# A new order for every engine's work in a fused attention and gated-FFN kernel, with each engine's line of tasks taken strictly in turn

## The chip, the cores and the metric

The kernel runs on one core of a Trainium2 chip. The core has a matrix engine (TensorE, PE; its weight loads are shown apart as PEld), a vector engine (VectorE, DVE), a scalar engine (ScalarE, ACT), a general engine (GpSimd, POOL) and an engine that here only issues DMAs (SyncE, SP). The metric is the device time of one execution in microseconds; a lower time is better.

## The reference

```python
def _attn_ref(q, k, v, centroids):          # q, k, v: 4 x 8 x 768 x 64; centroids: 8 x 16 x 64
    q_n, k_n, c_n = (each row divided by its norm + 1e-06)
    q_assign = np.argmax(np.einsum('bhsd,hcd->bhsc', q_n, c_n), axis=-1)
    k_assign = np.argmax(np.einsum('bhsd,hcd->bhsc', k_n, c_n), axis=-1)
    mask = q_assign[:, :, :, None] == k_assign[:, :, None, :]
    scores = 1 / np.sqrt(D) * np.matmul(q, k.transpose(0, 1, 3, 2))
    scores = np.where(mask, scores, -1000000000.0)
    attn = softmax(scores)                  # with the maximum taken off, sum + 1e-09
    return np.matmul(attn, v)

def reference(...):
    x = attn_out.transpose(0, 2, 1, 3).reshape(3072, 512)
    gate = 1.0 / (1.0 + np.exp(-(x @ w_gate)))     # w_gate, w_val: 512 x 1536
    return gate * (x @ w_val) @ w_out              # w_out: 1536 x 512
```

(Each line that stands for several is shortened.) Every query and key belongs to the nearest of 16 centroids of its head; a query attends to the keys of its own centroid. The result, 3072 tokens of 512 values, goes through a gated feed-forward layer.

## The kernel before

**Attention.** The eight heads are taken as four pairs `p` for each of the four batches `b`. Queries and keys of a pair are loaded in their natural layout (`nat`), turned on PE or DVE into `t` (`t32`), and scored against the centroids (`scored`, L794 on PE); DVE finds the best centroid of each token, and a one-hot mask (`oh`, `oht`) is copied by SP's DMAs into rows beside the turned values in `even` and `odd` (one tile for the even, one for the odd half of the blocks; POOL casts the values into them in L757, and SP copies a part of one to the other in L761). So one matmul of 80 rows (L1114, `score`) gives a score that already carries the mask. For each group of score blocks PE writes scores into two PSUM banks, ACT takes the exponential of both (L1138, `exponentials`, into `es`), and PE multiplies them with the values and a column of ones (L1165, `value`). DVE divides by the sums (L1190 `rec`, L1195 `norm`, into `xn`), and the block is turned into `x` either on PE or by a DMA transposition that SP issues (L1223, `turn_by_dma`).

**Feed-forward.** As soon as a group of 384 tokens has all its pairs, the feed-forward products on it are interleaved with the attention of the next groups. Part of the products with `w_gate` and `w_val` is plain (L1506), part goes through a scheme of seven products for a 2 x 2 block multiplication (`seven_products`, L1584), with sums on DVE (L1615, L1631) and copies and gate functions on ACT (L1603, L1622). The gated values are in `hT`. The product with `w_out` (`project`) also uses seven products (L1375): DVE forms sums of `hT` (L1345), ACT halves some results (L1393, `half` and `diff`), DVE combines a product with one of these into the output tile (L1400, `summed`), and SP or ACT stores the tile (a DMA of L441). In the last group of the program the last product is split in two halves of columns, copied out by ACT (L1393) and DVE (L684) and stored apart.

**Buffers.** The eight PSUM banks are one pool, `ring`: any task that needs a bank or a pair gets one that is free by the plan. `nat` has nine buffers, `es` and `xn` four each, `x`, `hT`, `gt` and `out2` two each. Which buffer a task gets is settled in the plan too; a task that takes a buffer waits for the last users of it.

**What sets the order.** The program is built once as a list of 2390 tasks (`Order.add`): each is a small piece of work on one engine, with the tasks it depends on and the buffers it takes. `Order.run` gives each task its place from a table of numbers (`PLACES`) and each of the 198 DMAs a time from issue to landing that the plan is to count with (`LANDINGS`). `Order.schedule` then plans all engines on one clock: again and again it takes, of all engines, the task that can start first; among the tasks of an engine that could start within 0.02 us of each other it takes the one with the lowest place. The tasks are emitted in that order, and each engine works through its own instructions in the order in which they were emitted, waiting where an input or a buffer isn't ready. No time of the plan is used on the chip; only the orders and the choice of buffers are.

```python
first = min(c[0] for c in cand)
start, t = min(
    (c for c in cand if c[0] <= first + 0.02), key=lambda c: (c[1].due, c[0])
)
if best is None or start < best[0]:
    best = (start, t)
```

For the kernel before, this choice gives on every engine the order of the numbers in `PLACES`.

Of the kernel before, what the change touches and what calls it, by code (L numbers as in the profile page):

```python
# [18 lines left out]
107 121 225 233 263 268 495 255 502 7 22 24 26 30 25 29 35 41 28 33 38 46 34 39 44 50 42 48 53 57 61 64 65 70 76 78  # L19
81 86 45 51 49 55 54 59 56 62 63 68 77 85 75 89 94 100 134 140 142 145 148 166 156 84 110 88 114 95 122 119 129 127  # L20
138 144 153 141 155 162 176 186 189 192 202 207 213 226 124 131 161 174 164 180 183 191 188 197 205 215 201 217 224
234 240 246 251 254 258 264 266 103 109 116 198 187 267 190 270 222 278 248 282 250 291 271 295 279 304 285 312 275
286 297 305 319 325 321 384 389 403 407 357 368 381 411 415 423 445 451 458 468 476 484 328 367 380 418 336 426 434
441 344 450 457 470 525 543 532 538 514 521 530 536 551 561 629 631 556 563 571 576 636 656 652 661 669 675 680 681
660 666 671 677 683 687 695 704 707 688 691 718 700 66 67 69 73 102 71 72 74 79 104 80 82 83 87 106 90 91 93 96 112
120 125 130 98 99 105 132 108 111 113 137 117 118 123 139 126 128 136 149 133 135 143 160 146 147 152 175 200 203
209 150 151 154 157 158 159 163 212 167 168 170 171 172 173 185 214 223 230 235 177 179 181 182 194 236 193 195 196
199 204 237 206 208 210 211 216 239 245 249 252 218 219 220 221 227 253 228 229 231 232 238 256 241 242 243 244 247
262 269 273 283 287 257 259 260 261 265 281 272 274 276 277 280 293 288 289 290 292 294 314 320 322 335 340 353 360
480 488 352 358 366 378 382 386 385 400 399 410 404 416 412 422 421 432 433 442 443 453 454 466 467 477 481 490 489  # L30
496 500 507 506 511 522 528 529 535 534 539 537 542 541 548 546 555 553 560 559 566 296 298 299 300 301 302 306 331
307 308 309 310 311 313 315 332 339 342 347 317 318 323 348 327 329 333 349 337 338 341 359 343 345 351 365 355 356
362 377 361 363 369 383 387 396 401 370 372 373 374 375 376 379 402 388 390 391 392 393 394 398 409 414 420 430 395
397 405 429 406 408 413 431 417 419 425 440 424 427 435 452 437 438 446 465 447 449 455 479 483 486 491 459 460 461
462 463 464 469 497 471 472 473 474 475 478 482 498 501 504 516 519 485 487 492 512 493 494 499 513 503 505 508 520
509 510 515 527 517 518 523 533 524 526 531 540 544 547 552 558 549 569 612 620 568 575 574 580 595 602 630 637 640
647 648 653 625 644 645 650 579 585 587 606 605 611 621 627 658 670 686 690 668 678 673 685 682 694 703 716 693 720
698 725 679 696 689 705 711 724 722 730 573 582 588 591 594 596 598 600 603 570 608 614 618 717 727 729 731 736 734
742 744 751 758 756 762 769 774 784 795 738 753 743 766 772 773 782 778 796 783 797 805 806 814 813 820 827 833 818
931 793 807 810 816 856 865 881 872 890 878 891 899 901 909 915 920 945 957 925 963 632 659 676 646 639 684 649 654  # L40
662 672 713 697 721 726 749 732 699 701 708 712 746 747 785 789 706 715 942 759 798 935 841 857 866 874 885 889 861
# [82 lines left out]
2.47 2.47 2.57 2.47 2.47 2.47 2.47 2.484 2.95 2.95 2.95 2.95 2.95 2.95 2.95 3 2.95 2.95 2.95 2.95 2.95 2.95 2.95  # L124
2.95 2.919 2.9 2.47 2.52 2.484 2.47 2.484 2.47 2.47 2.47 2.8 3.064 2.8 2.8 4.1 4.264 4.1 4.1 3.07 3.204 2.8 2.85 2.8
2.8 4.17 4.17 4.63 4.77 3.07 3.07 3.07 3.07 2.8 2.8 2.8 2.8 3.598 3.07 2.8 2.8 2.8 4.694 4.3 3.07 3.237 3.07 2.735
2.735 2.895
"""


# [1692 lines left out]
```

## Time and profile before

| what | before |
|---|---|
| median of 3 runs | 311.02 us (309.73 to 311.69) |
| profiled execution | 309.38 us, span 307.6 us |
| PE busy | 299.2 us, 97% of the span |
| ACT busy | 259.0 us, 84% |
| DVE busy | 249.3 us, 81% |
| POOL busy | 79.2 us, 26% |
| granted TensorE clock | 1.000 over the span |
| HBM traffic | 28.87 MB read, 6.29 MB written |

The profile is that of one execution; its span runs from the first to the last event that the profiler saw, and the execution's own time is 1.78 us longer. A busy time counts an engine's instructions, so an engine that waits is idle; matmuls overlap in a pipeline and their ends are modelled, so a busy PE can still hide short stalls. Lines are those of the kernel before. In rows of instructions, `out<-in` names the tiles written and read, with the numbers of their buffers left out.

### The profile page before, as it was taken

To read this page: it belongs to the slowest core of one execution; us is meant where nothing else is said; L and a number is where in the kernel's file an instruction comes from. 1 tells how busy PE (TensorE), PEld (TensorE's weight loads), DVE (VectorE), ACT (ScalarE), POOL (GpSimd) and SP (SyncE) were. 2 spreads that over 40 slices of the span, in tenths; PEclk is the share of its full clock that TensorE was granted. 3 is DMA by queue.
4 is the path that set the end of the run, shared out by engine and by line. 5 is a ranking of instruction groups with operands and counts; after the bars stand their busy time and mean duration, and the time that the engine had idled before them with its cause. 6 is when DMAs were issued, how large, how long until landed. Compare 5 with 4: busy or idle time off the path is not lost.

```text
span 307.6 us, 8905 instructions
## 1 busy us (share of the span) xinstructions
PE 299.2 (97%) x3491; PEld 237.5 (77%) x3491; DVE 249.3 (81%) x604; ACT 259.0 (84%) x449; POOL 79.2 (26%) x112
## 2 busy tenths in 40 slices
PE   7998899999999999999999999999999999999994
PEld 3676588754468688977998779987998889988974
DVE  4999996897886687889789989979778738964993
ACT  4898799884448899999999989999999998995841
POOL 5898849741022033600001301470000000000000
PEclk9999999999999999999999999999999999999999
DMA  6999999994557595931384674893210120131003
GB/s 222 368 287 181 218 202 145 181 137 85 97 90 160 111 128 166 118 47 22 84 134 90 104 119 118 178 124 29 71 37 26 40 61 34 25 74 70 0 3 136
DMA packets 97833, 34.79 MB, mean 113 GB/s; under 512 B 83152, under 2 KB 93568, under 8 KB 97792
## 3 DMA queue, kind: packets, MB, share of 16 engines
q1 hardware_dynamic: 72192, 24.57, 34.6%
q0 software_dynamic: 24880, 8.92, 29.2%
q10 hardware_dynamic: 720, 0.75, 0.7%
q8 instruction: 27, 0.44, 0.6%
q14 instruction: 14, 0.11, 0.1%
HBM read 28.87 MB, written 6.29 MB: 114 GB/s over the span
## 4 chain that ended last, share of the span: by engine, by line
PE 89%; ACT 4%; DVE 3%; DMA 2%; issue 1%; ACTq 0%; SPq 0%
PE ring L1584 25%; PE ring L1114 19%; PE ring L1375 18%; PE ring L1506 11%; PE ring L1165 10%; ACT es L1138 3%; PE ring L794 3%; DMA nat<-in_q_dram 1%; PE ring L902 1%; DVE hT L1631 1%; DMA out<-in_centroids_dram 1%; DVE t L684 1%; PE ring L942 1%; DVE even L681 0%; ACT t L909 0%
## 5 line engine op out<-in xcount | busy, mean ns | idle before, releaser
L1138 ACT ACTIVATE es<-ring,nbias 128x768 f16<-128x768 f32 (+1 forms) x189 | 169.8, 941 | 15.1 <-PE ring L1114 10.5
L1165 PEld LDWEIGHTS <-es 128*128 128x128 f16 x1152 | 51.3, 97 | 11.7 <-ACT es L1138 0.8
L1165 PE MATMUL ring<-vp,es 128*128 128x65 f16 x1152 | 56.6, 193 | 0.0
L757 POOL CAST even<-t 128x768 f16<-128x768 f32 x24 | 21.1, 892 | 116.3 <-issue 37.3
L1615 DVE TENSOR_TENSOR nat<-ring,nat 128x384 f32<-128x384 f32 x68 | 36.7, 552 | 14.9 <-ACT nat L1603 8.6
L1622 ACT ACTIVATE nat<-nat 128x384 f32<-128x384 f32 x68 | 37.3, 575 | 1.9 <-DVE nat L1615 1.9
L1584 PEld LDWEIGHTS <-wss 128*128 128x128 f16 x408 | 34.8, 98 | 2.2 <-issue 0.2
L1603 ACT COPY nat<-ring 128x384 f32<-128x384 f32 x68 | 33.9, 519 | 2.7 <-PE ring L1584 1.7
L1584 PE MATMUL ring<-nat,wv 128*128 128x192 f16 x272 | 32.6, 246 | 0.0
L1584 PE MATMUL ring<-nat,wss 128*128 128x192 f16 x272 | 32.4, 246 | 0.0
L1584 PE MATMUL ring<-x,wg 128*128 128x192 f16 x272 | 32.3, 246 | 0.2 <-DVE hT L1631 0.2
L1375 PEld LDWEIGHTS <-hT 128*128 128x128 f16 x294 | 27.2, 97 | 4.9 <-DVE hT L1631 0.4
L1375 PE MATMUL ring<-wo,hT 128*128 128x256 f16 x216 | 29.0, 272 | 0.1
L1114 PE MATMUL ring<-even 80*128 80x384 f16 (+2 forms) x120 | 26.4, 294 | 0.9 <-ACT es L1138 0.6
L1114 PE MATMUL ring<-even,odd 80*128 80x384 f16 (+2 forms) x120 | 26.8, 293 | 0.0
L1114 PE MATMUL ring<-odd 80*128 80x384 f16 x96 | 26.5, 325 | 0.1
L1114 PE MATMUL ring<-odd,even 80*128 80x384 f16 x96 | 26.4, 326 | 0.2 <-ACT es L1138 0.2
L1584 PEld LDWEIGHTS <-wv 128*128 128x128 f16 x272 | 23.3, 97 | 3.0 <-issue 0.2
L1114 PEld LDWEIGHTS <-even 80*128 80x128 f16 x216 | 19.5, 98 | 7.1 <-issue 3.5
L1114 PEld LDWEIGHTS <-odd 80*128 80x128 f16 x216 | 19.3, 98 | 6.6 <-issue 4.5
L1584 PEld LDWEIGHTS <-wg 128*128 128x128 f16 x272 | 23.1, 98 | 1.5 <-issue 0.4
L1506 PE MATMUL ring<-x,wg 128*128 128x256 f16 (+2 forms) x112 | 22.5, 326 | 0.1
(120 smaller groups left out, 519.0 us busy)
## 6 DMA issues: line engine op xcount, KB each, us to landing
out_dram<-out SPq DMA_DIRECT2D x22, 256.0 KB, 2.4
nat<-in_k_dram SPq DMA_DIRECT2D x32, 96.0 KB, 3.1
nat<-in_q_dram SPq DMA_DIRECT2D x32, 96.0 KB, 3.0
odd<-even SPq DMA_DIRECT2D x12, 192.0 KB, 3.5
vp<-in_v_dram POOLq DMA_DIRECT2D x24, 96.0 KB, 5.2
nat<-in_k_dram SPq DMA_DIRECT2D x5, 384.0 KB, 6.2
nat<-in_q_dram SPq DMA_DIRECT2D x5, 384.0 KB, 5.7
nat<-in_v_dram SPq DMA_DIRECT2D x4, 384.0 KB, 7.2
```

The lines of the kernel that those rows point to most:

```text
L684: nc.vector.tensor_scalar(to, of, by, None, ALU.mult)
L757: nc.gpsimd.tensor_copy(t[:, NM[nm], cols], t32[p, nm].tile[:, cols])
L794: nc.tensor.matmul(out=ps[32 * g : 32 * g + 32, half, :QB], lhsT=cblk[:, 2 * p + half, :], rhs=t32[p, nm].tile[:, half * QB : (half + 1) * ...
L1114: nc.tensor.matmul(out=to, lhsT=kb.tile[0:80, 0, e * QB + j // 2 * 128 : e * QB + (j // 2 + 1) * 128], rhs=qb_.tile[0:80, 1, e * QB + c0 * ...
L1138: i = nc.scalar.activation(to, of, AF.Exp, bias=nbias, scale=D ** -0.5 if quarters(b, p) else scale,).ins
L1165: nc.tensor.matmul(out=av.tile[:, g : g + D + 1], lhsT=es.tile[:, i * N + c * 128 : i * N + (c + 1) * 128], rhs=vp[:, e, j, :], start=firs ...
L1375: nc.tensor.matmul(out=ps[:, lo:hi], lhsT=left_()[:, i], rhs=right(i)[:, lo:hi], start=new and i == 0, stop=i == NFC // 2 - 1, skip_group_ ...
L1506: nc.tensor.matmul(out=ps[:, :N], lhsT=ws[fc // FPG][:, dcc, fc % FPG, :], rhs=xb.tile[:, dcc, :N], start=(dcc == 0), stop=(dcc == NDC - 1),)
L1584: nc.tensor.matmul(out=ps[:, f], lhsT=w_[:, d, f], rhs=x_()[:, d], start=new and not (f or d), stop=d == 1, skip_group_check=True,)
L1603: nc.scalar.copy(held(i), bank(r_))
L1615: lambda: nc.vector.tensor_tensor(held(i), bank(r_), held(i), ALU.add), deps,
L1622: lambda: nc.scalar.activation(held(i), held(i), AF.Tanh, scale=0.5), [m], due_ffn(work), lat=0.16,
```

## The change

The two tables are replaced, and three additions in `Order.schedule` let an engine take only the task that is next in its own line, sorted by `PLACES`; the choice by planned start is left only between engines. The numbers of `PLACES` come from a search over such orders in the plan, in which half of the weight was on plans with randomly lengthened transfers; `LANDINGS` holds new times for the plan. No task, instruction or buffer is added or taken away.

```diff
 PLACES = """
 0 1 9 2 16 3 5 10 11 13 14 15 17 19 20 32 36 4 8 6 12 18 21 23 27 92 97 31 37 40 101 115 43 47 52 165 169 58 178 184
-107 121 225 233 263 268 495 255 502 7 22 24 26 30 25 29 35 41 28 33 38 46 34 39 44 50 42 48 53 57 61 64 65 70 76 78
+107 121 214 233 257 282 493 289 455 7 22 24 26 30 25 29 35 41 28 33 38 46 34 39 44 50 42 48 53 57 61 64 65 70 76 78
...
         free = {e: 0.7 for e in {t.eng for t in self.tasks}}
+        line = {e: deque() for e in free}
+        for t in sorted(self.tasks, key=lambda t: t.due):
+            line[t.eng].append(t)
         order, under_way, pool, twin = [], {"SP": [], "POOL": []}, (0.0, 0.0), (0.0, 0.0)
         while any(wait.values()):
             best = None
             for e, ts in wait.items():
                 cand = []
                 for t in ts:
+                    if t is not line[e][0]:
+                        continue
                     r = t.ready
...
             wait[t.eng].remove(t)
+            line[t.eng].popleft()
             now = max(t.ready, free[t.eng])
```

The code of the tasks stays as it was; its lines have moved by four (L1400 before is L1404 in the changed kernel, L1114 is L1118, L441 is L445). On every engine the order is the same in the two kernels up to about 24 us of the profile of before; behind that 413 of PE's 1048 tasks, 354 of DVE's 584, 105 of ACT's 453, 51 of POOL's 107 and 150 of SP's 198 have another place, most on PE and ACT by one or two.

Three places show how. The first is PE's line at about 28 us: transpositions by `ident` (L724, changed L728), scores (L1114, changed L1118) and values (L1165, changed L1169). Before:

```order
L1114 LDWEIGHTS odd2_82
L1114 MATMUL ring_121<-even2_76,odd2_82 128x256
L724 MATMUL ring_121<-ident_124,nat4_65 128x128 x3
L724 MATMUL ring_121<-ident_124,nat5_66 128x128 x3
L1165 LDWEIGHTS es3_98
L1165 MATMUL ring_121<-vp2_142,es3_98 128x65
```

Changed:

```order
L728 MATMUL ring_121<-ident_124,nat4_65 128x128 x3
L1118 LDWEIGHTS even3_77
L1118 MATMUL ring_121<-even3_77 128x256
L1118 LDWEIGHTS even3_77
L1118 MATMUL ring_121<-even3_77 128x256
L1118 LDWEIGHTS even3_77
L1118 MATMUL ring_121<-even3_77 128x256
L1118 LDWEIGHTS odd3_83
L1118 MATMUL ring_121<-even3_77,odd3_83 128x256
L728 MATMUL ring_121<-ident_124,nat5_66 128x128 x3
L1169 LDWEIGHTS es3_98
L1169 MATMUL ring_121<-vp2_142,es3_98 128x65
```

The four scores of the next block (`even3`, `odd3`) now stand between the two transpositions and ahead of the values of `es3`; before they followed those values.

The second is SP's line at about 125 us: masks copied from `oht` into `even` and `odd`, DMA transpositions of the normalized blocks `xn` (L1223, changed L1227), and copies of `even` into `odd` (L761, changed L765). Before:

```order
L441 DMA even2_76<-oht0_86 16x768
L441 DMA odd3_83<-oht0_86 16x768
L441 DMA even2_76<-oht0_86 16x768
L1223 DMA_TRANSPOSE x1_107<-xn2_104 128x3x128
L761 DMA odd4_84<-even5_79 64x1536
L761 DMA odd5_85<-even4_78 64x1536
```

Changed:

```order
L1227 DMA_TRANSPOSE x1_107<-xn0_102 128x3x128
L1227 DMA_TRANSPOSE x1_107<-xn2_104 128x3x128
L445 DMA odd3_83<-oht0_86 16x768
L445 DMA even3_77<-oht0_86 16x768
L445 DMA even2_76<-oht0_86 16x768
L1227 DMA_TRANSPOSE x1_107<-xn1_103 128x3x128
L445 DMA even3_77<-oht0_86 16x768
L765 DMA odd4_84<-even4_78 64x1536
```

All eight masks stood ahead of the transposition of `xn2` before; now four of them stand behind it.

The third is the end of DVE's line: the last sums of `hT` (L1345, changed L1349), the sums into the output tile (L1400, changed L1404) and the last copy. Before:

```order
L1345 TENSOR_TENSOR hT1_109<-hT1_109 128x3x128
L1400 SCALAR_TENSOR_TENSOR out20_112<-ring_121,half0_117 128x256
L1345 TENSOR_TENSOR hT1_109<-hT1_109 128x3x128
L1400 SCALAR_TENSOR_TENSOR out21_113<-ring_121,nat4_65 128x256
L1400 SCALAR_TENSOR_TENSOR out20_112<-ring_121,diff0_118 128x256
L1400 SCALAR_TENSOR_TENSOR out21_113<-ring_121,nat4_65 128x256
L684 TENSOR_SCALAR out21_113<-ring_121 128x128
```

Changed:

```order
L1349 TENSOR_TENSOR hT1_109<-hT1_109 128x3x128
L1349 TENSOR_TENSOR hT1_109<-hT0_108,hT1_109 128x3x128
L1349 TENSOR_TENSOR hT1_109<-hT1_109 128x3x128
L1404 SCALAR_TENSOR_TENSOR out20_112<-ring_121,diff0_118 128x256
L1404 SCALAR_TENSOR_TENSOR out21_113<-ring_121,nat4_65 128x256
L1404 SCALAR_TENSOR_TENSOR out20_112<-ring_121,half0_117 128x256
L1404 SCALAR_TENSOR_TENSOR out21_113<-ring_121,nat4_65 128x256
L688 TENSOR_SCALAR out21_113<-ring_121 128x128
```

The sum with `half0`, and the one of `out21` that stood behind it, complete two output tiles of 256 KB; they have moved behind the sums with `diff0` and with the other `nat4`. The stores on SP keep their order.

204 rows, old and new, of tables (LANDINGS, PLACES) are left out of this document.

## The prediction

> **What bounds the kernel now.** I read the page first: the busy shares, the clock, and the chain of work that ended last.
>
> ```profile
> span 307.6 us, 8905 instructions
> PE 299.2 (97%) x3491; PEld 237.5 (77%) x3491; DVE 249.3 (81%) x604; ACT 259.0 (84%) x449; POOL 79.2 (26%) x112
> PEclk9999999999999999999999999999999999999999
> PE 89%; ACT 4%; DVE 3%; DMA 2%; issue 1%; ACTq 0%; SPq 0%
> ```
>
> TensorE is busy for 299.2 of 307.6 us at a clock that never falls, and 89% of the chain is its own work. No matmul is added or removed, so a new order can only change the 8.4 us in which PE is idle, and whatever stalls hide inside "busy". Where the idle time lies comes from the busy time of each stretch (columns: time, PE, PEld, DVE, ACT, POOL with the count of instructions, then the clock, the DMA share, GB/s).
>
> ```profile
> 24.00:42.00 18.00, 16.02 (x230) 12.00 (x229) 16.86 (x48) 14.98 (x18) 13.60 (x18) 1.00 1.12 204
> 42.00:120.00 78.00, 78.00 (x833) 54.61 (x832) 61.34 (x147) 60.37 (x96) 24.69 (x31) 1.00 0.97 134
> 120.00:240.00 120.00, 119.77 (x1507) 101.81 (x1504) 104.28 (x235) 115.60 (x213) 20.46 (x25) 1.00 0.58 86
> 240.00:296.00 56.00, 55.90 (x655) 48.56 (x654) 41.14 (x93) 47.49 (x92) 1.41 (x2) 1.00 0.16 42
> 296.00:308.00 12.00, 7.75 (x75) 6.57 (x73) 6.77 (x23) 2.59 (x7) 0.00 (x0) 0.99 0.25 87
> ```
>
> The order is the same in both kernels up to about 24 us. From there to 296 us PE is idle for 1.98 + 0.00 + 0.23 + 0.10 = **2.31 us** in all: that is about what a better order can win. The last 12 us hold 4.25 us without PE work, the drain of the last outputs. So three places decide: 24 to 42 us, the long dense middle, and the drain.
>
> **24 to 42 us.** First what PE waits for there, then the rounds behind it (timeline: start, length, engine, line, operation, and in brackets the idle time before it).
>
> ```profile
> PE ring L1114 <- ACT es L1138: 0.8, 2, 0.6
> PE ring L724 <- DVE t L684: 0.5, 1, 0.5
> PE ring L724 <- ACT es L1138: 0.3, 1, 0.3
> ```
>
> ```profile
> 26.53 2.12 ACT L1138 ACTIVATE es<-ring,nbias 128x1024 f16<-128x1024 f32 x2
> 28.41 0.65 PE L1165 MATMUL ring<-vp,es 128*128 128x65 f16 x16
> 28.89 0.49 PE L1114 MATMUL ring<-even 80*128 80x256 f16 x3
> 29.59 1.11 ACT L1138 ACTIVATE es<-ring,nbias 128x1024 f16<-128x1024 f32 x1 [0.95 <-PE ring L1114]
> 31.45 1.11 ACT L1138 ACTIVATE es<-ring,nbias 128x1024 f16<-128x1024 f32 x1 [0.74 <-PE ring L1114]
> 33.25 3.49 ACT L1138 ACTIVATE es<-ring,nbias 128x1024 f16<-128x1024 f32 x4 [0.69 <-PE ring L1114]
> ```
>
> An exponential (L1138) reads two PSUM banks, the next score products (L1114) write two, and the next exponential needs those. The pair ends at 28.65, but PE does transpositions and value products (L1165) first and begins the scores at 28.89. The changed PE line puts these four scores ahead of a transposition and of the values. In the round behind, the exponential ends at 31.45 + 1.11 = 32.56 and ACT's next one starts 0.69 later; that loop stays. So the scores can begin some 0.05 behind the exponential, at 28.70, which is **0.2 us** earlier, once: the following rounds are the same loop and shift with it. DVE now does several block placements before a reciprocal and a normalization here (sums of 0.2 to 0.6 us each), which can eat the gain. Bounds: +0.2 if DVE's copies become the late input, and -1.98 if all of PE's idle time in the stretch went. I take -0.2, nearest to the one round that the rows show to be shortened.
>
> **The dense middle, 42 to 296 us.** Here most moved places lie: pairs of neighbours on PE and ACT, sums and weight sums on DVE, loads, masks and stores on SP, casts and loads on POOL.
>
> ```profile
> L1615 DVE TENSOR_TENSOR nat<-ring,nat 128x384 f32<-128x384 f32 x68 | 36.7, 552 | 14.9 <-ACT nat L1603 8.6
> PEld L1165 <- ACT es L1138: 0.8, 3, 0.3
> ```
>
> The first row is DVE's largest group, with 14.9 us of idle time in front of it: DVE waits for others here, and an exchange of two sums costs nothing as long as that slack is there. ACT has 4.40 us left in 120 to 240 us, by the stretch above. I cost all swaps of the middle, moved DMAs included, at **0**: PE's 78.00 of 78.00 and 119.77 of 120.00 us are the cover, eight banks let it run ahead, and where the cover is gone the delay shows one to one as PE idle there. Below zero the bound is the 0.33 us that PE idles here, with another 0.8 us in which a weight load waited for an exponential (second row, 120 to 240 us): -1.1. Upwards the bound comes from the rival on SP below, +3.2. I take 0, since the nearest rows show neither a wait to remove nor one that must arise.
>
> **The drain.** Here the order moves something on the path itself. The timeline of the last microseconds:
>
> ```profile
> 300.52 0.42 DVE L1400 SCALAR_TENSOR_TENSOR out<-ring,half 128x256 f32<-128x256 f32 x1
> 300.97 3.45 SPq L441 DMA_DIRECT2D out_dram<-out  x4
> 301.20 0.42 DVE L1400 SCALAR_TENSOR_TENSOR out<-ring,nat 128x256 f32<-128x256 f32 x1
> 301.79 0.42 DVE L1400 SCALAR_TENSOR_TENSOR out<-ring,diff 128x256 f32<-128x256 f32 x1 [0.16 <-PE ring L1375]
> 302.44 0.42 DVE L1400 SCALAR_TENSOR_TENSOR out<-ring,nat 128x256 f32<-128x256 f32 x1 [0.23 <-PE ring L1375]
> 303.12 0.38 ACT L1393 ACTIVATE out<-ring 128x256 f32<-128x256 f32 x1 [2.25 <-PE ring L1375]
> 303.85 0.92 ACTq L441 DMA_DIRECT2D out_dram<-out  x2
> 304.10 0.29 DVE L684 TENSOR_SCALAR out<-ring 128x128 f32<-128x128 f32 x1 [1.23 <-ACT out L1393]
> ```
>
> SP's four stores leave at 300.97, 301.66, 302.90 and 304.09:
>
> ```profile
> 301.66 0.33 SPq L441 DMA_DIRECT2D out_dram<-out  x1
> 302.90 0.33 SPq L441 DMA_DIRECT2D out_dram<-out  x1
> 304.09 0.33 SPq L441 DMA_DIRECT2D out_dram<-out  x1
> ```
>
> The first two (256 KB each) wait for the L1400 sums of 300.52 and 301.20. In the changed DVE line those two stand behind the sums of 301.79 and 302.44, and the last of these cannot start earlier, since it waits for PE. So: 302.44 + 0.42 = 302.86; the two sums, 0.42 each, end at about 303.3 and 303.7; SP's first store leaves at about 303.35 instead of 300.97. The others stand behind it; now the first two leave 0.69 us apart (300.97, 301.66), with 0.33 us of issue each: at 0.5 us apart, an estimate between these, they leave at 303.85, 304.35 and 304.85, the last one 0.76 later than now. PE's last products do not wait for the moved sums. Some of the additions (L1345) ahead of them come up to 0.3 us sooner or later, and one matmul that starts 0.16 us earlier is given back two matmuls on.
>
> What the stores then cost (first GB/s in 40 slices of 0.225 us from 299 on, then the amount, then from issue to landing):
>
> ```profile
> GB/s 0 0 0 0 0 0 0 0 0 0 0 0 200 382 346 373 373 410 246 0 5 296 273 9 0 209 410 355 310 285 180 0 0 0 0 0 0 0 0 0
> DMA packets 864, 1.05 MB, mean 117 GB/s; under 512 B 96, under 2 KB 480, under 8 KB 864
> DMA to landing us min/median/max: 1.7/2.0/2.1
> ```
>
> Now the stores come in three bursts with gaps; the last issue, 304.42, lands at 304.42 + 2.0 = 306.4, 1.2 before the end of the span. With the new order all 1.05 MB goes out in one. By issue alone the last landing is 304.85 + 2.0 = 306.9, **+0.5**. By bytes: the first data follow the issue by some 0.8 us (300.97, and the thirteenth slice at 301.70 to 301.93), so from 304.2 on; at the mean of the five full slices, 377 GB/s, 1.05 MB take 2.8 us, until 307.0, and the last landing comes 0.4 behind the last bytes (306.0 and 306.4 now): 307.4, **+1.0**. I take **+0.9**, nearer to the bytes, because a store of 256 KB takes 0.7 us at 377 GB/s and three of them come within 0.5 us of each other (SP's two and ACT's first, at about 303.5); the ends are 0.4, if a little of the order of issue is regained, and 1.3, if the issues stand 0.69 apart.
>
> The Trainium skill, "DMA: Bandwidth & Descriptors", section "Issuing engines are not separate DMA queues", says that DMAs started by different engines run on the same 16 DMA engines and interleave. By it the two stores of ACT's queue add no rate, and the sum goes by bytes, +1.0; without it they would not count in that stream, and the issue alone, +0.5, would hold. The trace agrees as far as it goes: the second burst has both queues in flight and also peaks at 410 GB/s. The same page's "Anatomy of one DMA — SWDGE (gpsimd) path" gives, for DMAs of another issuer, about 2.0 us plus the bytes at 436 GB/s; for the whole burst that is an estimate of 4.4 us from 303.35 on, 307.75, +1.4, while the 2.0 us measured for the last stores are a little below its figure.
>
> **Sum.** -0.2 + 0 + 0.9 = +0.7. The profiled execution took 309.38 us, 1.78 more than its span, so 310.1 for such a run. It lies 1.64 us below the median of the runs shown, 311.02 (309.73 to 311.69); against the median I predict **311.7 us**.
>
> **Rivals.**
> (1) *The stalls go* (faster). For it speaks that ACT idles 0.95, 0.74 and 0.69 us in the rounds above, and that DVE's placements there move. Against it: each round is closed by its own banks, and the middle has nothing to give. All of 24 to 42 us and all of the middle's -1.1, with the drain at +0.4, give 309.38 - 1.98 - 1.1 + 0.4 = 306.7, or 308.3 against the median: 0.9% at best; beyond 1% it needs stalls inside "busy" that no row shows. Chance of more than 1%: 0.13.
>
> (2) *A line that must wait* (slower). Place: SP at 126 us. Four copies of masks from `oht` left SP ahead of the transposition of a normalized block; now they stand behind it.
>
> ```profile
> 124.34 0.56 DVE L1195 TENSOR_TENSOR xn<-ring,rr 128x384 f16<-128x384 f32 x1
> 125.41 0.59 SPq L441 DMA_DIRECT2D even<-oht  x1
> 126.11 1.19 SPq L1223 DMA_TRANSPOSE x<-xn  x1
> 135.28 0.32 PE L1114 MATMUL ring<-even 80*128 80x384 f16 x1
> DMA to landing us min/median/max: 1.8/2.4/5.9
> ```
>
> On DVE two L1615 sums (552 ns each) are put ahead of that normalization: it ends at 124.90 + 1.1 = 126.0, the transposition, 1.19 long, is out of SP's way at about 127.3, and the third mask leaves some 1.3 later (0.59 each and a little between), at 128.6, landing at 131.0 with the median of 2.4. The scores that use it begin at 135.28, so 4.3 us are spare. It decides when the mask lands behind 135.28: with the longest landing, 5.9, and a normalization 4 us later, it lands at 138.5, PE stands 3.2 us, which ACT, with 4.40 us of slack in these 120 us, does not give back to PE, and the time is 309.38 + 0.7 + 3.2 = 313.3, or 314.9 against the median. The same build (a transposition ahead of masks or loads) comes back at several other places of SP's line, and POOL has one cast ahead of weight loads; that makes it likelier than one place would. Chance: 0.29.
>
> (3) *The drain is hidden* (the change does nothing there): if DMA rates let the stores catch up, +0.4 at the least, and with -0.2 the time is 309.6, 311.2 against the median. It stays within the forecast's band.
>
> **Chances and range.** Forecast with (3): 0.58, its own range 310.6 to 313. About 1% (3.1 us) is what a measurement of this kernel can tell from no change. Faster 0.13, within it 0.58, slower 0.29. The range goes from 308.3 (rival 1) to 315 (rival 2).
>
> **What would show it.** After: the two L1400 sums at 303 us or later and SP's stores from 303.3 on, one burst in GB/s, the end about 1 us further behind PE's last matmul; the L794 block that starts after the rounds some 0.2 us earlier; PE still at 78.0 and 119.5 or more in the two middle stretches. PE idle there of a microsecond or more, ended by a DMA or by ACT, proves rival 2; less than 1 us idle in 24 to 42 proves rival 1. A longer run with the same PE rows would make my sum wrong as a whole.

## The result

| | before | changed |
|---|---|---|
| median | 309.82 us (22 runs, 309.49 to 311.69) | 310.75 us (22 runs, 309.92 to 313.89) |
| ratio | | **1.0035**, 95% interval 1.0018 to 1.0052 |
| profiled execution | 309.38 us, span 307.6 | 310.81 us, span 309.0 |

The changed kernel is 0.35% slower, some 1.1 us. The predicted difference was +0.7 us; the absolute 311.7 us stood on the median of three runs, which lay 1.2 us above that of 22. The changed kernel's runs lie wider apart than those of before.

The page of the changed kernel, the lines that answer to those shown of before:

```profile
span 309.0 us, 8870 instructions
PE 299.2 (97%) x3491; PEld 238.5 (77%) x3491; DVE 251.6 (81%) x604; ACT 259.4 (84%) x449; POOL 79.6 (26%) x112
PE 82%; DVE 8%; DMA 4%; ACT 3%; issue 2%; SPq 0%; ACTq 0%; DVEq 0%
```

PE works as long as before, 299.2 us. DVE and DMA have a larger share of the chain, which is where work waits for them. The stretches (columns as above):

```profile
24.00:42.00 18.00, 15.93 (x229) 12.25 (x227) 17.46 (x47) 14.86 (x17) 12.86 (x18) 1.00 1.17 210
42.00:120.00 78.00, 77.68 (x824) 54.30 (x822) 61.08 (x145) 60.34 (x95) 22.49 (x28) 1.00 0.87 125
120.00:240.00 120.00, 119.81 (x1517) 102.47 (x1514) 106.29 (x237) 115.79 (x213) 23.67 (x28) 1.00 0.66 89
240.00:296.00 56.00, 55.91 (x660) 48.55 (x658) 41.15 (x94) 48.11 (x93) 1.41 (x2) 1.00 0.18 47
```

Busy time says little here: the second stretch lost 0.32 us, the others changed by 0.1 at most. What tells more is when the same work starts. Three of the blocks that score against the centroids (L794 before, L798 after), before and then changed:

```profile
35.42 1.50 PE L794 MATMUL ring<-t,cblk 128*32 128x384 f32 x16
104.28 1.50 PE L794 MATMUL ring<-t,cblk 128*32 128x384 f32 x16
177.85 1.50 PE L794 MATMUL ring<-t,cblk 128*32 128x384 f32 x16
```

```profile
35.83 1.50 PE L798 MATMUL ring<-t,cblk 128*32 128x384 f32 x16
105.05 1.50 PE L798 MATMUL ring<-t,cblk 128*32 128x384 f32 x16
178.11 1.50 PE L798 MATMUL ring<-t,cblk 128*32 128x384 f32 x16
```

The changed kernel is 0.41 us late at 35 us, 0.77 at 104 us, and only 0.26 at 178 us. So the middle was not neutral: it lost time and won some back. To follow this over the whole program I set the start of PE's n-th matmul in one profile against that of the n-th in the other (the numbers in the next table are such differences, in us, in one profiled execution each; a minus is ahead of before):

| place in before | changed | 1: end put back | 5: and load moved | 9: load moved, same banks | 12: start only |
|---|---|---|---|---|---|
| 25 us | +0.16 | +0.33 | +0.22 | +0.37 | +0.37 |
| 45 us | +0.41 | +0.33 | | +0.47 | +0.82 |
| 60 us | +0.41 | +0.34 | +0.18 | +0.46 | +0.82 |
| 75 us (in 5: 70) | +0.77 | +1.61 | +0.21 | +0.39 | +0.86 |
| 115 us (in 5: 100) | +0.78 | +1.61 | +0.11 | +0.40 | +0.97 |
| 195 us (in 5: 200) | +0.24 | +1.08 | -0.42 | -0.19 | +1.07 |
| 215 us (in 5: 210) | +0.32 | +1.16 | 0.00 | -0.11 | +2.56 |
| 295 us (in 5: 290) | +0.17 | +1.01 | 0.00 | -0.28 | +2.56 |

Then comes the drain. The changed kernel:

```profile
301.93 0.42 DVE L1404 SCALAR_TENSOR_TENSOR out<-ring,diff 128x256 f32<-128x256 f32 x1 [0.88 <-PE ring L1379]
302.40 1.54 PE L1379 MATMUL ring<-nat,hT 128*128 128x256 f16 x18
302.64 0.42 DVE L1404 SCALAR_TENSOR_TENSOR out<-ring,nat 128x256 f32<-128x256 f32 x1 [0.29 <-PE ring L1379]
302.98 0.42 DVE L1404 SCALAR_TENSOR_TENSOR out<-ring,half 128x256 f32<-128x256 f32 x1
303.31 0.41 DVE L1404 SCALAR_TENSOR_TENSOR out<-ring,nat 128x256 f32<-128x256 f32 x1
303.42 2.45 SPq L445 DMA_DIRECT2D out_dram<-out  x4
```

PE's last matmul ends at 302.40 + 1.54 = 303.94, 5.06 us before the end of the span. Before, the group that the page of before shows in the same place ended 3.84 us before the end:

```profile
302.27 1.49 PE L1375 MATMUL ring<-nat,hT 128*128 128x256 f16 x18
```

The drain is 1.22 us longer, and that is most of the 1.4 us between the two spans; 0.16 us of the rest is there at 25 us already, where the orders have hardly begun to differ.

### The profile page after: what moved, and what is told of

Same layout as the page of the kernel before. It is cut to its first block, busy times and chain, and to the rows that moved or that the text cites. A ratio compares the mean times of both kernels' runs of the same rounds, so it can differ in the third digit from the quotient of the medians.

```text
span 309.0 us, 8870 instructions
## 1 busy us (share of the span) xinstructions
PE 299.2 (97%) x3491; PEld 238.5 (77%) x3491; DVE 251.6 (81%) x604; ACT 259.4 (84%) x449; POOL 79.6 (26%) x112
## 4 chain that ended last, share of the span: by engine, by line
PE 82%; DVE 8%; DMA 4%; ACT 3%; issue 2%; SPq 0%; ACTq 0%; DVEq 0%
PE ring L1588 25%; PE ring L1379 18%; PE ring L1118 17%; PE ring L1169 9%; PE ring L1510 9%; DMA x<-xn 3%; ACT es L1142 2%; PE ring L798 2%; DVE even L685 1%; DMA nat<-in_k_dram 1%; DVE odd L685 1%; DVE t L660 1%; DVE mx L667 1%; DVE t L688 1%; DVE hT L1635 1%
## 5 line engine op out<-in xcount | busy, mean ns | idle before, releaser
L1169 PEld LDWEIGHTS <-es 128*128 128x128 f16 x1152 | 53.5, 97 | 12.2 <-ACT es L1142 0.4
L1169 PE MATMUL ring<-vp,es 128*128 128x65 f16 x1152 | 58.9, 193 | 0.5 <-ACT es L1142 0.3
L761 POOL CAST even<-t 128x768 f16<-128x768 f32 x24 | 21.4, 915 | 114.8 <-PE ring L1118 41.8
L1626 ACT ACTIVATE nat<-nat 128x384 f32<-128x384 f32 x68 | 36.6, 570 | 1.6 <-DVE nat L1619 1.4
L1118 PE MATMUL ring<-even 80*128 80x384 f16 (+2 forms) x120 | 26.8, 294 | 1.4 <-ACT es L1142 0.7
L1118 PE MATMUL ring<-even,odd 80*128 80x384 f16 (+2 forms) x120 | 27.3, 293 | 0.2 <-ACT es L1142 0.2
L1118 PE MATMUL ring<-odd,even 80*128 80x384 f16 x96 | 26.9, 326 | 0.2 <-ACT es L1142 0.2
L1118 PE MATMUL ring<-odd 80*128 80x384 f16 x96 | 26.7, 325 | 0.1
L1118 PEld LDWEIGHTS <-even 80*128 80x128 f16 x216 | 19.4, 98 | 6.7 <-issue 3.8
L1118 PEld LDWEIGHTS <-odd 80*128 80x128 f16 x216 | 19.0, 98 | 6.8 <-issue 4.9
L1677 ACT ACTIVATE gt<-ring 128x256 f32<-128x256 f32 (+2 forms) x28 | 13.7, 500 | 12.2 <-PE ring L1510 9.1
```

The costliest lines, as they stand in the source:

```text
L761: nc.gpsimd.tensor_copy(t[:, NM[nm], cols], t32[p, nm].tile[:, cols])
L1118: nc.tensor.matmul(out=to, lhsT=kb.tile[0:80, 0, e * QB + j // 2 * 128 : e * QB + (j // 2 + 1) * 128], rhs=qb_.tile[0:80, 1, e * QB + c0 * ...
L1169: nc.tensor.matmul(out=av.tile[:, g : g + D + 1], lhsT=es.tile[:, i * N + c * 128 : i * N + (c + 1) * 128], rhs=vp[:, e, j, :], start=firs ...
L1626: lambda: nc.scalar.activation(held(i), held(i), AF.Tanh, scale=0.5), [m], due_ffn(work), lat=0.16,
L1677: lambda rg=rg, gt=gt: nc.scalar.activation(take(gt)[:, :N], rg.tile[:, :N], AF.Tanh, scale=0.5),
```

## The experiments

Ratios are to the kernel before, run beside each kernel on the same chip (its medians: 309.82 us in runs 1 to 4, 309.88 in 5 to 8, 309.69 in 9 to 12). Where an order is made from the tables of both kernels, the diff shows the rows that move, or says which order holds where.

**4. The rule alone.**

```diff
-PLACES, LANDINGS of the changed kernel
+PLACES, LANDINGS of the kernel before
 (the three additions to schedule stay)
```

> The changed code of the schedule with the two tables of before; every engine's instructions stand as in the kernel before. All theories: ratio 1.000 within 0.002; the width of its interval is what this comparison can tell. Rival (the rule itself does something): any other ratio.

Every instruction of every engine, and every choice of a bank or buffer, is that of the kernel before. Measured: 310.19 us (309.50 to 311.47), ratio 1.0019 (1.0006 to 1.0032). So the rule does nothing by itself, and a difference of 0.2% between two kernels of this kind is not yet a difference. Four of the twelve runs lie above 311.0 us, where one of 23 of the kernel before does. The profiled execution, 311.47 us and the longest of the twelve, shows one source of this: PE is 1.98 us late after the first 10 us, and stays 2.0 us late to the end. The same nine transpositions of keys on PE, in the kernel before and then in this one (shortest, median and longest in ns, then the first and last start in us):

```profile
L1010 PE MATMUL ring<-ident,nat x9: 272/272/333, 4.6 to 5.9; 128*128 128x128 f32 x9
```

```profile
L1014 PE MATMUL ring<-ident,nat x9: 421/421/476, 5.1 to 7.1; 128*128 128x128 f32 x9
```

They begin 0.54 us later, since a key load lands later (5.1 us instead of 4.55), and that is the smaller part. The larger is that PE's matmuls take half as long again here, 421 ns instead of 272 ns, and start 0.21 us apart instead of 0.11. The slower rate lasts to 9.5 us in this execution, and in that of the kernel before it ends ahead of 4.8 us. The trace's first record of the granted clock, which is 1.000, begins at 9.45 us here and at 4.00 us before, so the clock row of the page says nothing of the time ahead of it. Why it begins at different times in identical programs is open; in the other profiles here it begins between 3.4 and 6.2 us. All further readings of a profile are therefore taken from 25 us on, or stretch by stretch.

**2. The end alone**, on the kernel before:

```diff
 L1349 TENSOR_TENSOR hT1<-hT1
-L1404 SCALAR_TENSOR_TENSOR out20<-ring,half0
 L1349 TENSOR_TENSOR hT1<-hT1
-L1404 SCALAR_TENSOR_TENSOR out21<-ring,nat4
 L1404 SCALAR_TENSOR_TENSOR out20<-ring,diff0
 L1404 SCALAR_TENSOR_TENSOR out21<-ring,nat4
+L1404 SCALAR_TENSOR_TENSOR out20<-ring,half0
+L1404 SCALAR_TENSOR_TENSOR out21<-ring,nat4
```

> The kernel before, with nothing but the end of DVE's and ACT's lines in the order of the changed kernel. Theory drain: 1.0 to 1.3 us slower than before, ratio 1.003 to 1.004, SP's first store near 303.3, one burst. Rival early: no change, 0.999 to 1.001.

Measured: 311.00 us (310.67 to 311.16), ratio 1.0036 (1.0023 to 1.0049), 1.2 us. (ACT's last copy and the store ahead of it trade places as well.) PE keeps one and the same distance to before, 0.43 us, from 25 us to 300 us; the drain has what is lost:

```profile
302.75 1.49 PE L1379 MATMUL ring<-nat,hT 128*128 128x256 f16 x18
303.71 2.45 SPq L445 DMA_DIRECT2D out_dram<-out  x4
DMA to landing us min/median/max: 2.1/2.9/3.2
```

The span is 309.2 us, so 4.96 us lie behind PE's last matmul, 1.12 more than before. Two sums of 0.42 us, put behind two that wait for PE, cost 1.1 us of the program.

**1. The end put back**, on the changed kernel, the same piece the other way round:

> The changed kernel, with the end of DVE's and ACT's lines (the last six tasks of DVE, the last copy and store of ACT) put back into the order of before. Theory drain (the whole loss is the stores that leave SP late in one burst): SP's first store leaves near 301.1 instead of 303.4, the end comes 1.0 to 1.3 us sooner, ratio to before 0.999 to 1.001. Rival early (the loss comes from the 0.4 to 0.8 us that PE falls behind before 65 us and carries to the end): the time stays within 0.3 us of the changed kernel, ratio 1.002 to 1.004.

A miss in the time: 311.07 us, ratio 1.0034 (1.0007 to 1.0061), with runs from 308.81 to 313.23. The drain did what was expected: PE's last group, 1.49 us long, starts at 303.25 in a span of 308.7, which leaves 3.96 us, 1.1 less than in the changed kernel. But PE lost 1.27 us between 60 and 75 us (table), and the view of PE's waits from 58 to 66 us says for what; first the changed kernel, then this one:

```profile
PE ring L1510 <- DMA x<-xn: 0.3, 1, 0.3
DMA to landing us min/median/max: 4.6/7.8/9.2
```

```profile
PE ring L1510 <- DMA x<-xn: 1.2, 1, 1.2
DMA to landing us min/median/max: 4.9/7.9/9.8
```

PE waits there for a DMA transposition of `xn` into `x`. The second row of each is the time from issue to landing of those from 44 to 66 us. What stands around it, before and changed:

```profile
52.19 1.21 SPq L1223 DMA_TRANSPOSE x<-xn  x1
52.90 1.51 POOL L441 DMA_DIRECT2D wo<-in_moe_w_out_dram  x2
DMA to landing us min/median/max: 5.2/5.8/6.6
```

```profile
51.26 2.94 SPq L1227 DMA_TRANSPOSE x<-xn  x2
50.08 0.99 POOL L445 DMA_DIRECT2D wo<-in_moe_w_out_dram  x1
53.21 0.87 POOL L445 DMA_DIRECT2D wo<-in_moe_w_out_dram  x1
```

Before, both loads of `w_out` (512 KB each) were issued behind the transposition; in the changed order one of them goes out 1.2 us ahead of the first of the pair, and the transpositions land up to 9.2 and 9.8 us after their issue instead of 6.6. The medians do not add up: the end alone costs 1.2 us (run 2) and all the rest 1.3 (this run), but both together some 1.1. How often long runs come differs from kernel to kernel, as run 4 shows, so a median alone doesn't settle what a part is worth.

**5. That load moved back**, together with the end, in POOL's line:

```diff
-L445 DMA wo2_138<-in_moe_w_out_dram
 L445 DMA nat5_66<-in_k_dram
 L445 DMA vp0_140<-in_v_dram
 L445 DMA vp4_144<-in_v_dram
 L445 DMA wo0_136<-in_moe_w_out_dram
+L445 DMA wo2_138<-in_moe_w_out_dram
```

> The first experiment (changed order, end of before) with one more task moved on POOL: the load of the third chunk of w_out stands behind that of the second again, as before, instead of nine places ahead. Theory load: in the changed order this 512 KB load goes out at 50 us, ahead of the DMA transposition that SP issues at 52.6, the transposition lands 9 to 10 us after its issue instead of 5, and PE waits 0.4 to 1.3 us for it near 61 us, a different time in each run. Then the wait is gone here, PE is at most 0.3 us behind the kernel before at 65 us and ahead of it by 0.3 to 0.6 at 295 us; ratio 0.9965 to 0.9985, and the runs lie closer together than those of the first experiment. Rival masks (the spread comes from the masks on SP near 126 us): PE is not late at 65 us in either, the runs spread as before, ratio 1.000 to 1.004.

Measured: 309.80 us, eleven of twelve runs between 309.40 and 310.09 and one at 313.29; ratio 1.0002 (0.9982 to 1.0023). The wait at 61 us is gone (+0.18 at 60 us, +0.21 at 70), the transpositions land in 6.5 us at most, and the runs lie closer, as the theory of the load has it. The gain is smaller than expected, though. At 200 us PE is 0.42 us ahead of before, at 210 us level with it, and a wait stands between, in 200 to 208 us:

```profile
PE ring L1118 <- ACT es L1142: 0.4, 1, 0.4
```

Moving one load in the tables moves the plan's clock, and 283 tasks got another PSUM bank than in the changed kernel.

**9. The load moved without the banks:**

```diff
         order = self.schedule()
+        load = self.tasks[48]
+        order.remove(load)
+        order.insert(order.index(self.tasks[46]) + 1, load)
```

> As the first experiment (changed order, end of before), and the load of the third chunk of w_out is again issued behind that of the second, but this time only where the tasks are emitted, so that every PSUM bank stays the one of the changed kernel (in the fifth experiment the plan, and with it 283 choices of buffers, had moved too). Theory banks (the 0.4 us that PE lost at 204 us in the fifth experiment came from the other choice of banks): no wait of PE at 61 us and none at 204 us, PE 0.4 to 0.6 us ahead of before at 295 us, ratio 0.9975 to 0.9990. Rival (PE waits at 204 us whenever it arrives early, since ACT is the limit there): PE level with before from 205 us on, ratio 0.9995 to 1.0005.

Measured: 309.30 us (308.73 to 310.57), ratio 0.9982 (0.9961 to 1.0003). No wait at 61 us, none from 200 to 208 us, PE 0.28 us ahead at 295 us and 0.65 ahead if one counts from 25 us. That is the theory of the banks. Other runs bear it out: from 200 to 210 us PE loses 0.42 and 0.43 us with the banks of run 5 (runs 5 and 8), and 0.08 to 0.11 with those of the changed kernel (the changed kernel, runs 1, 7, 9 and 10), also in run 7, which is 0.50 us ahead there; so an early arrival isn't what costs. The load is the other half: runs 1 and 9 differ in nothing else, and their intervals (1.0007 to 1.0061 and 0.9961 to 1.0003) lie apart. Against before, the interval still touches 1.

**8 and 10. The split store**, on the kernels of 5 and of 9:

```diff
-        store(1, 0, DM, [c21, c22], "ACT" if end else "SP")
+        if end:
+            store(1, HM, DM, [c22])
+            store(1, 0, HM, [c21], "ACT")
+        else:
+            store(1, 0, DM, [c21, c22])
```

> As the kernel with both parts put back (end of DVE's and ACT's lines, load of w_out), and the 256 KB store of ACT at the end is split: the half that is ready at 302.2 leaves on SP at about 302.3, and only 128 KB remain for ACT at 303.9. Theory bytes: the last burst holds 256 KB instead of 384 KB, the end comes 0.2 to 0.35 us sooner than in that kernel; ratio 0.9955 to 0.998. Rival issue: no difference to that kernel.

> The same with the split store of the eighth experiment. Theories bytes and banks together: another 0.3 us less than the kernel without the split, ratio 0.9965 to 0.998, the fastest kernel here. Rival: as the eighth, 0.9985 to 0.999.

Measured: 309.38 us (308.98 to 310.01), ratio 0.9989 (0.9981 to 0.9998) for 8, and 309.05 us (308.36 to 310.37), ratio **0.9975** (0.9955 to 0.9994) for 10, the fastest kernel here, faster than both. Set against what identical programs showed in run 4, 0.25% is little more than that. In the profile the step is clear. In 8, PE's last group starts at 302.51 and ends at 304.00, in a span of 307.4: 3.4 us instead of 3.84 (3.9 in run 5), and the last stores land sooner after their issue than the 2.0 us of before:

```profile
302.51 1.49 PE L1379 MATMUL ring<-nat,hT 128*128 128x256 f16 x18
DMA to landing us min/median/max: 1.6/1.8/2.1
```

The last three stores are issued 0.10, 0.34 and 0.67 us behind PE's last matmul in runs 5 and 8 alike, but the last lands 2.63 us behind it in 5 and 2.30 in 8 (2.64 and 2.30 in 9 and 10). The issues did not move against PE, the bytes in front of them did: theory bytes.

**7. Fewer bytes**, on the changed kernel (three quarters of two output tiles are left out):

```diff
-            store(0, 0, DM, [c11, c12])
+            store(0, 0, DM // 4, [c11, c12])
...
-        store(0, 0, DM, [c11, c12])
+        store(0, 0, DM // 4 if end else DM, [c11, c12])
```

> The changed kernel, but the two 256 KB stores that leave late at the end move only a quarter of their columns (64 KB each), so three quarters of these two tiles are left out of the output; the issues stay where they are. Theory bytes: the last burst is 0.39 MB shorter, which at 377 GB/s is 1.0 us, so the last landing comes 0.8 to 1.1 us sooner. Rival issue (what counts is when the last store is issued, and its 2 us): the last landing moves by less than 0.2 us.

Inconclusive as built. 309.25 us, ratio 0.9986 (0.9970 to 1.0002), and 3.6 us behind PE's last matmul instead of 5.06. But a quarter of the columns needs only the sum that was ready early, so the two stores left before the burst and their issues moved as well as their bytes: from 302 us on, SP issued two stores in the place of four. Bytes and issue are told apart by 8 and 10, not by this. Up to the end, though, this run has the order and the banks of the changed kernel, and so it is a second profile of them: PE gains 0.07 us from 25 to 45 us and is 0.57 us ahead of before at 295 us. The load of `w_out` stands ahead here too (49.8 us), and the transposition lands 7.9 us after its issue, but it was issued at 52.0, landed at 59.9, and PE did not wait for it.

**6. The load alone**, on the kernel before, ahead of the key loads at 49 us (the plan gave 43 tasks another bank):

```diff
+L445 DMA wo2_138<-in_moe_w_out_dram
 L445 DMA nat4_65<-in_k_dram
...
-L445 DMA wo2_138<-in_moe_w_out_dram
```

> The kernel before with only that load of w_out moved ahead, to the place in front of the key loads at 49 us. Theory load: the transposition that SP issues at 52.2 lands at 60 us or later instead of 57.4; PE, which starts the product at 60.8, waits 0 to 1.5 us; ratio 1.000 to 1.005, with a wider spread than before's. Rival masks: lands as before, ratio 1.000.

Measured: 309.96 us, ratio 1.0007 (0.9988 to 1.0026), eight runs from 309.64 to 310.14 and two at 311.49 and 312.43. In the profile the transposition took 6.1 us to land, at 59.0, and PE, 0.2 us late throughout, did not wait. The two long runs fit the theory, but no profile shows one. In the order of before this load, at 49.0 us nearly 4 us ahead of the transposition (52.8), costs nothing in the median.

**11. The masks behind the transposition**, on the kernel before, the rival of the prediction in its own place:

```diff
-L445 DMA odd3_83<-oht0_86
-L445 DMA even3_77<-oht0_86
-L445 DMA even2_76<-oht0_86
-L445 DMA even3_77<-oht0_86
 L1227 DMA_TRANSPOSE x1_107<-xn2_104
+L445 DMA odd3_83<-oht0_86
+L445 DMA even3_77<-oht0_86
+L445 DMA even2_76<-oht0_86
+L445 DMA even3_77<-oht0_86
```

> The kernel before with only SP's line at 126 us changed: four of the eight copies of masks stand behind the transposition, as in the changed kernel; no bank changes. Theory of the prediction (4 us are spare): ratio 1.000 within 0.0015, PE shows no new wait at 135 to 140 us. Rival (the masks decide): a wait of 0.5 us or more there, ratio 1.0015 or more.

Measured: 309.63 us, ratio 1.0002 (0.9980 to 1.0024), no new wait at 135 to 140 us (PE +0.73 us at 125 us and +0.74 at 140 us). The masks cost nothing, but not for the margin that I gave:

```profile
127.55 1.86 SPq L445 DMA_DIRECT2D even<-oht  x3
DMA to landing us min/median/max: 1.9/6.4/7.0
136.02 0.32 PE L1118 MATMUL ring<-even 80*128 80x384 f16 x1
```

The last of the three leaves at about 128.8 and lands 6.5 us later (median 6.4, longest 7.0), 0.7 us before the scores start. In the kernel before the masks at this place, issued from 121.0 to 125.4 us, landed in 1.8 to 4.4 us.

The profile of this run also has, in the order of before, the wait of the changed kernel (view of PE's waits from 58 to 66 us):

```profile
PE ring L1510 <- DMA x<-xn: 0.3, 1, 0.3
```

SP was late there and issued the transposition at 53.2 us, behind the first load of `w_out` (52.4) and with the second; it landed 8.7 us later, and PE went from +0.30 to +0.74 us. So the order is one way to put a load in front of this transposition, and a late SP is another.

**3. The middle alone**: the changed order between 120 and 300 us only.

```diff
 order of each engine:
-  changed kernel
+  before, for tasks that started before 120 us
+  changed kernel, for tasks that started from 120 to 300.4 us
+  before, for the rest
```

> The order of before for all tasks that started before 120 us, then that of the changed kernel up to 300.4 us, then the end of before. Theory: the middle of the changed kernel wins back 0.6 us of PE time between 130 and 240 us (0.77 us behind at 120 us, 0.17 us behind at 295 us), and if those are stalls removed there and not only slack that absorbs a late start, this kernel is 0.4 to 0.6 us faster than before, ratio 0.998 to 0.9985. Rival (slack only: a late start is absorbed where PE waits anyway for something with a clock of its own): no change, 0.9995 to 1.0005.

A miss: 311.15 us, ratio 1.0047 (1.0035 to 1.0059). PE stands at +0.26 us at 120 us, -0.19 at 135 and +1.05 at 140; the changed kernel shows the same dip (+0.92, +0.43, +0.73), since the n-th matmuls are not the same ones there, so the loss around 137 us is 0.8 us, 0.7 of it in one wait (view of PE's waits from 134 to 142 us):

```profile
PE ring L798 <- ACT es L1142: 0.7, 1, 0.7
```

The banks were planned anew across the seam. From 140 to 195 us PE then wins back 0.41 us (0.49 in the changed kernel), but the time of this run does not tell whether the middle gains on its own; runs 5, 9 and 10 do (below).

**12. The start alone**: the changed order up to 35.5 us, then that of before.

```diff
 order of each engine:
-  before
+  changed kernel, for tasks that started before 35.5 us
+  before, for the rest
```

> The changed order for the tasks that started before 35.5 us, that of before for all others (banks are planned anew, so only the stretch up to 42 us is judged). The prediction's step: PE 0.2 us ahead at 37 us, measured from where it stands at 24 us. Rival (a normalization that DVE does 0.5 us later holds a value product, since both use the bank of the sums): 0.1 to 0.4 us behind.

Measured: 311.83 us, ratio 1.0065 (1.0042 to 1.0088). From 25 to 45 us PE falls 0.45 us behind, which is the rival's sign and a little over its size. The larger loss comes later, 1.5 us between 195 and 215 us, where the order is that of before but 310 tasks have another PSUM bank (PE's waits from 190 to 212 us; the kernel before has none there):

```profile
PE ring L1118 <- ACT es L1142: 0.8, 2, 0.6
PE ring L1118 <- DVE nat L1619: 0.3, 1, 0.3
```

A late arrival is not the reason: runs 11 and 4 have the order and the banks of before and come there 0.7 and 2.0 us late, and they lose 0.04 us at most.

## Why the prediction was right, and where it was not

**The whole.** A small loss from the end of the program was forecast, +0.7 us and inside 1%, and +0.35% was measured. The three terms were -0.2, 0 and +0.9; the profile has +0.25 (25 to 45 us), -0.24 (45 to 295 us) and +1.22. Only the third came about as worked out; that the other two add up to nothing in this execution is luck (in run 7, with the same order up to the end, they are -0.07 and -0.69).

**The drain** was right in its mechanism and too small in its size. The issues came as worked out: SP's first store at 303.42 (303.35 predicted), the last at 304.8 (304.85). The burst:

```profile
GB/s 0 0 0 0 0 0 0 0 0 0 0 0 0 0 0 0 0 0 55 300 419 373 382 400 373 346 391 364 301 326 326 273 32 0 0 0 0 0 0 0
L445 SPq DMA_DIRECT2D out_dram<-out x4: 333/416/1049, 303.4 to 304.8; - x4
DMA to landing us min/median/max: 2.1/2.9/3.2
```

1.05 MB take 3.05 us, from 304.25 to 307.3, or about 340 GB/s, where I had put the 377 GB/s of full slices; the slices of the small stores (64 and 128 KB) at the end have 273 to 326 GB/s. The last store lands 2.9 us after its issue, at 307.7, instead of 2.0. The step that was mis-sized is "at the mean of the five full slices": 307.4 predicted, 307.7 measured. Of the +1.2 where I took +0.9, the last landing has 1.1, set against PE's last matmul (which came 0.2 us later than before), and 0.1 lies between that landing and the end of the span. By bytes alone I had +1.0, so part of what is missing is that I went below it, towards the issue. The sixth store was in flight with five others of two queues, no slice is above 419 GB/s (before, 419 too), and the median landing is 2.9 us behind its issue where it was 2.0. The Trainium skill's "DMA: Bandwidth & Descriptors" says under "Issuing engines are not separate DMA queues" that DMAs of different issuers run on the same engines and interleave; the trace agrees. (The burst with both queues and 410 GB/s that the prediction calls the second is the third.) The estimate from the fixed cost and rate that the same page of the Trainium skill gives under "Anatomy of one DMA — SWDGE (gpsimd) path", 307.75, came nearest; for stores from SP and ACT it is a figure of another issuer that happens to fit.

**The start** came out with the other sign in the profile of the changed kernel; at its best, elsewhere, it gave half of what I had put. The step that failed is "the scores can begin some 0.05 behind the exponential, at 28.70, which is 0.2 us earlier, once". The scores did begin sooner behind their exponential, 0.15 us instead of 0.24 (29.30, with the exponential pair over at 27.03 + 2.12 = 29.15), where I had put 0.05. In every profile with this order ACT idles 0.84 us before its next exponential instead of 0.95: so the new order is worth 0.1 us there, not 0.2. And in the changed kernel the exponentials themselves were late:

```profile
23.52 0.56 DVE L1199 TENSOR_TENSOR xn<-ring,rr 128x384 f16<-128x384 f32 x1
...
26.20 0.28 DVE L1199 TENSOR_TENSOR xn<-ring,rr 128x128 f16<-128x128 f32 x1
26.53 0.65 PE L1169 MATMUL ring<-vp,es 128*128 128x65 f16 x16 [0.18 <-DVE ohf L956]
27.03 2.12 ACT L1142 ACTIVATE es<-ring,nbias 128x1024 f16<-128x1024 f32 x2 [0.33 <-PE ring L1169]
29.30 0.49 PE L1118 MATMUL ring<-even 80*128 80x256 f16 x3 [0.55 <-ACT es L1142]
```

The same two normalizations before:

```profile
23.13 0.56 DVE L1195 TENSOR_TENSOR xn<-ring,rr 128x384 f16<-128x384 f32 x1
...
25.67 0.28 DVE L1195 TENSOR_TENSOR xn<-ring,rr 128x128 f16<-128x128 f32 x1
```

The second normalization ends at 26.48 (before: 25.95). The value products that open the next block take over the bank that it reads, and start 0.05 later; PE's wait is put down to the small DVE write (L956) that ends just then. The exponential waits 0.33 us for those products, whose `es` buffer it is to fill; before, ACT ran from 23.37 for 5.28 us without a wait. So this round is held by a chain from DVE over PE to ACT, which my step left out: it looked at the exponential and the scores alone.

Why DVE is late there, 0.53 us, is known in its parts. 0.25 us are there at 17.9 us, before any of this. 0.14 come from one DVE operation at 20.8 us (L674, 0.90 us; before, L670, 0.75), which isn't the order: it also takes 0.88 us in run 11, which has the order of before here. The last 0.14 is the order: one placement moved from in front of a transposition (L656, changed L660) to behind it, and the same work between the first normalization and the second takes 2.09 us (24.11 to 26.20; 2.09 in run 1 too) instead of 1.95 (23.72 to 25.67; 1.94 in run 11). The reason that I had named ("DVE now does several block placements before a reciprocal and a normalization here", "which can eat the gain") fits this only in part: the several placements stand ahead of the next normalization, at 29.16 instead of 27.57 us, and PE does not wait for that one.

The wait of ACT comes and goes with how late DVE is. It is 0.33 us in the changed kernel, 0.17 to 0.36 in runs 8, 9 and 12, and absent in runs 1, 5, 7 and 10. The stretch from 25 to 45 us cost 0.25 us (changed), 0.12 (run 8), 0.10 (run 9) and 0.45 (run 12) with it, and 0.01, -0.02, -0.07 and -0.10 (runs 1, 5, 7, 10) without it. A gain of 0.2 is in none of them. What makes L674 longer in some executions stays open.

**The middle** came out near 0 by luck: two errors cancel. "I cost all swaps of the middle, moved DMAs included, at 0" failed at POOL's load of `w_out`, which cost 0.4 us in the profile of the changed kernel and 1.3 in that of run 1; runs 5, 8, 9 and 10, with the load moved back, have no such wait. It isn't there in every execution: run 7 has the load ahead and no wait. I had followed each moved DMA to its own user, and not asked what it stands in front of in the engines that all queues share. And rival 1's "the middle has nothing to give" failed too: from 115 to 195 us the changed order won 0.54, 0.53 and 0.59 us in the changed kernel, run 1 and run 9 (0.32 in run 10). It isn't a late start that is absorbed: with the order of before, runs 2, 4 and 11 keep their 0.43, 2.0 and 0.74 us through this stretch. Nor is it the banks: runs 5 and 8, with 283 others, won 0.54 and 0.53. PE's busy time in 120 to 240 us, 119.77 and 119.81 of 120, shows none of it: the stalls lie inside it, as the prediction said that they could, and I took no row of starts to look.

**Rival 2** stood at the right place with the wrong price. The masks did land late, 5.2 to 6.6 us after their issue in the changed kernel:

```profile
128.60 1.17 SPq L445 DMA_DIRECT2D even<-oht  x2
DMA to landing us min/median/max: 5.2/5.9/6.6
136.59 0.65 PE L1118 MATMUL ring<-even 80*128 80x384 f16 x3
```

The third mask, issued at 129.2, landed at 135.2; PE began these scores at 136.59. Of the 4.3 us that I had to spare 1.4 was left; the 2.4 us that I used was the median of all such copies, and here loads of `v` are in the queues. It did not decide, and run 11 confirms that. The same mechanism did decide at 61 us, with a load and a transposition, where I had not looked.

**Why the runs spread** is not settled. Moving the load back brought the runs of the changed order together (308.81 to 313.23 in run 1; 309.40 to 310.09 but for one run in 5; 308.73 to 310.57 in 9). That the long runs of the changed kernel are those in which PE waits longest at 61 us is argued from this; its one profile is of a run of 310.81 us. And there is a rival: run 4 has the program of before and still spreads from 309.50 to 311.47 us, the longest by 2 us lost at the start. What share of the long runs each has is not shown.

## What to carry to other kernels

A moved DMA is to be costed by what it delays in the shared DMA engines, not only by when its own data is needed, and a landing time is to be read from the rows of the same moment: a median over the program was off by 4 us here. Stores at the end should leave as their tiles get ready; work that only feeds a store is on the path as soon as the store is one of the last. And where a plan hands out buffers by its own clock, an edit of the plan can also change the buffers (it did in runs 3, 5, 6 and 12), so a comparison needs them held fixed.

## What the runs showed that I had not expected

The choice of PSUM banks alone went with a loss of 1.5 us in run 12 (195 to 215 us) and of 0.4 us in run 5 (200 to 210 us); the second went away when the banks were held fixed (run 9), the first was not tried so. Two identical programs (run 4) differed by 0.19% with an interval that excludes 1, so these intervals are too narrow for differences of that size; in the profiles, the 2.0 us between them arise within the first 10 us, most of it while PE's matmuls still run at the slower rate. And in the burst at the end SP's last issue of a store took 1.05 us instead of the 0.33 us of the others before.
